# Top-k attention and a Fourier-mixing MLP: the last batch's second chunk in seven products, its folds on one engine, and batch 1's folds spread over one step more

## The chip, the cores and the metric

The kernel runs on one core of a Trainium2 chip. TensorE (PE) multiplies matrices out of on-chip memory (SBUF) into accumulators (PSUM), VectorE (DVE), ScalarE (ACT) and GpSimd (POOL) work elementwise, and SyncE (SP) issues transfers between device memory and SBUF. Every engine takes its own instructions in order; semaphores order them against each other. The metric is the device time of one execution in microseconds. Six runs of the kernel before the change took 1929.75 to 1934.73 us, with a median of 1930.93.

## The reference

Eight batches, eight heads, 576 tokens, head size 64, all in float32; the model width is 8·64 = 512. A top-32 attention feeds a Fourier mixing and an MLP of width 2048:

```python
scores = scale * np.matmul(q, k.transpose(0, 1, 3, 2))
kth = np.partition(scores, -top_k, axis=-1)[..., -top_k:-top_k + 1]
scores = np.where(scores >= kth, scores, -1000000000.0)
attn = softmax(scores)                       # written out with max, exp, sum
x = (attn @ v), heads side by side           # (8, 576, 512)

X = np.fft.fft(np.fft.fft(x, axis=1), axis=2)
u = x + np.real(X)
un = (u - mean(u)) / np.sqrt(var(u) + 1e-06)
return u + np.maximum(un @ w_ch1, 0.0) @ w_ch2
```

## The kernel before, in words

**Steps.** The attention is cut into 288 items: 32 pairs of heads (four per batch), nine items per pair. An item is 128 rows (64 of each of two query tiles' tails in the fifth). A loop over steps `i` writes out every engine's instructions: in step `i` PE makes the scores of item `i+3` and transposes the masked exponentials of item `i-2` (`tpP`, L428); DVE finds the 32 largest of items `i` and `i+1` with MAX8 and MATCH_REPLACE8 (L384, L386); POOL turns the largest and the 32nd into two bounds (`nt`, L393); ACT makes a mask from them (L400), POOL subtracts it (L401), and ACT exponentiates (L407). `attend` (L465) multiplies by v; `to_tokens` transposes the result back (`tpx`, L505, in the single `o` bank of PSUM) and DVE normalises it into the batch's x tile (L509, L516). There are two buffers for x, so batch 2's first x tile waits until batch 0's results have been stored; `to_tokens` is held back in the plan until all four stores are issued.

**A plan by steps.** All that follows attention is put into the step loop by hand, with `at(step, where, function, cost)`. For each batch `T0` is a step two to four after the batch's last item. Then come:

- the folds (`fold_tails`, `fold_ops`): sums and differences of x by symmetry, so that the Fourier transforms are half as long. `fold_ops` has four parts for each parity of the frequency: sums over the token halves (`sd`, L597), over the channel halves (`zw`, L566), and two halves of `fg` (L550 to L562). Batch 0's run on DVE. Batches 1 to 6 fold on POOL (where "pool0"), batch 7 with parity 0 on DVE and parity 1 on POOL.
- the transform over tokens (`dft_tokens`, PE, `yp`, L629), one block for each parity at the steps `ft`; ACT copies it out to `y`.
- the transform over channels (`dft_channels`, PE, `mp`, L677) from step `fc` on, the sum with x, the statistics on DVE (L705, L706), the transposes to channels first (`tpu`, L742) and the inverse root (`rsqrt`).
- the batch's arrival: `mlp_units` puts the MLP into a queue as units. A unit of kind "hidden" multiplies by `w_ch1` (`hp`, L827), followed by a ReLU on ACT; one of kind "back" multiplies by `w_ch2`.

The step loop fills PE with units from that queue. `level` computes, at each arrival, a pace in estimated microseconds a step, such that the queue is empty at the next arrival; in each step units are taken out between the fixed pieces until the pace is met (`some`). The estimates come from `fixed_cost` and the units' costs.

**The MLP in two chunks.** A batch's 576 tokens make chunk 0 (two tiles of 128 and the 64 tail tokens, tile 4) and chunk 1 (tiles 2 and 3). For each tile of 128 the second product is sixteen matmuls 128x512 in eight units (`back`, `cp`, L854); the tails take four units (L893). Chunk 0 of batches 1 to 7 does not work that way. Its two tiles times `w_ch2` are a product of two-by-two blocks, and `fast` computes it with seven block products in place of eight (`p2, p1, p5, p4, p6, p3, p7`, banks `cv` and `cw`, L1025). The sums of blocks of the hidden activations are made by POOL in place (`mix`, L970), those of the weights once at the start, kept in device memory, and brought back over parts of `w_ch2` by SP (`bring`, L770). In the last batch `T4` and `T3` go into the buffers of the attention's `PT` tiles, and each product is added into x by DVE straight from PSUM (`to_x`, L983). `need` writes out a planned POOL sum at the latest where it is used; in the last batch every sum is written out at once.

In the last batch, attention is over when the folds start. What is left in the queue then are 15 units of batch 6's chunk 1.

Of the kernel before, what the change touches and what calls it, by code (L numbers as in the profile page):

```python
# [9 lines left out]
F32 = mybir.dt.float32  # L10
# [8 lines left out]
P = 128  # L19
# [45 lines left out]
def kernel(  # L65
# [9 lines left out]
    nc = tc.nc  # L75
# [10 lines left out]
    NIT = DF // P  # L86
# [9 lines left out]
    CHUNKS = ((0, 1, 4), (2, 3))  # L96
# [9 lines left out]
    attp = ctx.enter_context(tc.tile_pool(name="attp", bufs=2))  # L106
# [654 lines left out]
    DH = DM // 2  # L761
    NK = NIT // 2
# [4 lines left out]
    def bring(o, place, part):  # L767
        kcs = slice(NK // 2 * part, NK // 2 * (part + 1))
        dst = place[part] if isinstance(place, list) else place[:, kcs]
        nc.sync.dma_start(out=dst, in_=scr[:, o, kcs, :])  # L770
# [19 lines left out]
    sums, summed = [], set()  # L790
# [8 lines left out]
    def need(key):  # L799
        if key in summed:  # L800
            return

        kind = next(s[3] for s in sums if s[0] == key)
        for s in [s for s in sums if s[3] == kind]:
            sums.remove(s)
            s[2]()
            summed.add(s[0])
            if s[0] == key:
                break
# [3 lines left out]
    def mlp_units(b):  # L813
# [88 lines left out]
        def tails_done(cp, free):  # L902

            if b and not last:
                need((b, "x", 4))
            ct, rs = ct_of(4), rs_of[b]
            for h in range(2):
                r0 = TAIL + TH * h
                nc.scalar.copy(out=ct[TH * h:TH * (h + 1), :], in_=cp[r0:r0 + TH, :])

            def finish():
                xt, c = x[0:TAIL, 4, :], ct[0:TAIL]
                nc.vector.tensor_tensor(out=c, in0=cp[0:TAIL], in1=c, op=ALU.add)
                free()
                nc.vector.scalar_tensor_tensor(
                    out=xt, in0=c, scalar=rs[0:TAIL, 4:5], in1=xt, op0=ALU.mult, op1=ALU.add
                )
                for h in range(2):
                    tok = HS * h + 2 * P
                    nc.sync.dma_start(  # L920
                        out=out[b, tok:tok + TH, :], in_=x[TH * h:TH * (h + 1), 4, :]
                    )

            if last:
                finish()
            else:
                late_next.append(finish)

        def fast():

            ch = 0
            ta, tb = CHUNKS[ch][0], CHUNKS[ch][1]

            if last:
                second = [
                    attp.tile([P, NK // 2, DH], F32, name=f"w2_s_{n}", tag=f"PT{n}", bufs=1)
                    for n in range(2)
                ]
            else:
                second = w2_21  # L940

            def in_second(kc):
                half = NK // 2
                return second[kc // half][:, kc % half] if last else w2_21[:, kc]
            rs, banks = rs_of[b], {}
            lo, hi = slice(0, DH), slice(DH, DM)

# [10 lines left out]
            def later(key, us, fn, soon=False):  # L958

                n = sum(s[3] for s in sums) if soon else len(sums)  # L960
                sums.insert(n, ((b, *key), us, fn, soon))
                if last:
                    need((b, *key))

            def mix(dst, a, c, op=ALU.subtract):
                v = h()
# [85 lines left out]
                    mix("12", "12", "11")  # L1052

            def p5(part):
                need((b, "21", part))
                c = product("v", hi, "21", first, part, False)
                bring(T2, w2_12, part)
                if part:
                    to_x(tb, hi, c, 2)
# [6 lines left out]
                    mix("22", "22", "11")  # L1066

            def p6(part):
                need((b, "11", part))
                c = product("w", lo, "11", first, part, False)  # L1070
                bring(B12, w2_12, part)
                if part:
                    to_x(ta, hi, c, 4)

            def p3(part):
                need((b, "12", part))
                c = product("v", hi, "12", b22, part, False)
                if part:
                    to_x(ta, hi, c, None, lambda: (banks["v"][1](), store(ta)))

            def p7(part):
                need((b, "22", part))
                c = product("w", lo, "22", in_second, part, False)
                if not last:
                    bring(B21, second, part)
                if part:
                    to_x(tb, slice(0, DM), c, None, lambda: (banks["w"][1](), store(tb)))

            def begin():
# [2 lines left out]
                    if last:  # L1092
                        bring(T4, second, part)

            return [(0.0, begin, "hidden")], [
                (0.0, lambda: mix("21", "21", "22", ALU.add), "back")
            ] + [
                (1.75, lambda f=f, part=part: f(part), "back")
# [4 lines left out]
        for ch in range(2):  # L1103
            units += [
                (8 * CW[ch] / 1200.0, lambda ch=ch, it=it: hidden(ch, it), "hidden")
                for it in range(NIT)
            ]
            if b and ch == 0:
                begin, products = fast()
                units[1:1] = begin  # L1110
                units += products
            for t in (4,) if b and ch == 0 else CHUNKS[ch]:
                units += [
                    (1.75, lambda ch=ch, t=t, p=p: back(ch, t, p), "back")
                    for p in range(4 if t == 4 else 8)
                ]
# [42 lines left out]
    def at(step, where, fn, cost=0.0):  # L1159
        plan.setdefault((step, where), []).append(fn)  # L1160
        costs[step] = costs.get(step, 0.0) + cost
# [74 lines left out]
    for b in range(B):  # L1236
        end = PER_BATCH * (b + 1) - 1
        last = b == B - 1
        first, soon = b == 0, b == 1
        T0 = end + (2 if first else 3 if soon else 4)  # L1240
        if first:

            at(T0 - 1, "pool", lambda b=b: fold_tails(b, nc.gpsimd))

            def folds(b=b):
                for par, space in ((0, "own"), (1, "hT")):
                    for op in fold_ops(b, par, nc.vector, space):
                        op()
            at(T0, "dve", folds)
            ft, fc = (T0 + 1, T0 + 1), T0 + 1  # L1250
        elif soon:

            at(T0 - 1, "pool0", lambda b=b: fold_tails(b, nc.gpsimd))
            for par in range(2):
                def folds(par=par, b=b, T0=T0):
                    for n, op in enumerate(fold_ops(b, par, nc.gpsimd)):
                        at(T0 + 1 + 3 * par + n // 2, "pool0", op)
                at(T0, "begin", folds)
            ft, fc = (T0 + 3, T0 + 6), T0 + 7
        elif not last:  # L1260
            at(T0, "pool0", lambda b=b: fold_tails(b, nc.gpsimd))
            for par in range(2):
                def folds(par=par, b=b, T0=T0):
                    for n, op in enumerate(fold_ops(b, par, nc.gpsimd)):
                        at(T0 + (6 if par else 1) + n, "pool0", op)
                at(T0, "begin", folds)
            ft, fc = (T0 + 5, T0 + 11), T0 + 12
        else:
            at(T0 - 1, "pool0", lambda b=b: fold_tails(b, nc.gpsimd))

            def folds(b=b):
                a = fold_ops(b, 0, nc.vector)
                for op in a + fold_ops(b, 1, nc.gpsimd, "PT"):
                    op()
            at(T0, "dve", folds)
            ft, fc = (T0 + 1, T0 + 3), T0 + 4
        for par in range(2):
            at(ft[par], "pe1", lambda b=b, par=par: dft_tokens(b, par), 4.3)
        for n, t in enumerate((0, 1, 4, 2, 3)):
            quick = first or last  # L1280
            s = fc + (0 if first else n // 3 if last else n // 2)
            at(s, "pe2", lambda b=b, t=t, q=quick: dft_channels(b, t, q), 1.75)
            if not quick:
                at(s, "pool2", lambda b=b, t=t: add_mixed(b, t))
                at(s + 1, "dve", lambda b=b, t=t: stats(b, t))
            at(s + (1 if quick else 2), "pe", lambda b=b, t=t: channels_first(b, t), 0.6)
            if first and t == 4:
                at(s + 1, "pe", lambda: (queue.extend(waiting), waiting.clear()) and 0.0)
        at(s + 1, "begin" if quick else "dve", lambda b=b: rsqrt(b))
        arrivals.append(s + (1 if quick else 2))  # L1290
        at(arrivals[-1], "units", lambda b=b: (queue if b else waiting).extend(mlp_units(b)))
# [28 lines left out]
    def one_unit():  # L1320
        c, fn, _ = queue.pop(0)
        fn()
        return c
# [164 lines left out]
```

## Time and profile before

The profiled execution took 1930.82 us; the profile's span is 1929.0 us, so 1.8 us lie around it.

| | busy us | share of the span | instructions |
|---|---|---|---|
| PE | 1805.4 | 94% | 8960 |
| DVE | 1584.9 | 82% | 3262 |
| ACT | 1208.8 | 63% | 3078 |
| POOL | 871.4 | 45% | 1160 |

| stretch of the span, us | what runs there | PE idle, us |
|---|---|---|
| 320 to 505 | batch 1's attention, batch 0's MLP, batch 1's folds and transforms | 10.5 |
| 505 to 1748 | batches 2 to 7's attention beside the MLP of the batch before | 14.2 |
| 1748 to 1805 | batch 7's folds and transforms, the rest of batch 6's MLP | 5.0 |
| 1805 to 1929 | batch 7's MLP | 4.3 |

How to read what follows. A line of the chain gives start, length, engine, tile and line of a piece of the chain of work that ended last. A line in order of time gives start, length from the first to the last of a group, engine, line, operation, output and input tile, shape and count, and in brackets the idle time ahead of it with what ended it. A line of the windows gives a stretch, its length, the busy time of PE, PE's weight loads, DVE, ACT and POOL, then PE's granted clock as a share of full speed, the transfers' share and their GB/s. A line of the waits gives who waited for whom, the sum in us, how often, and the longest. A matmul in float32 stands in the records as two.

### The profile page before, as it was taken

What the parts mean: (1) busy time and instruction counts of PE and PEld (TensorE: products, weight loads), DVE (VectorE), ACT (ScalarE), POOL (GpSimd) and SP (SyncE); (2) the same over time, 40 slices, a digit from 0 to 9 for tenths busy, and PEclk for the clock granted to TensorE, in tenths of its full rate; (3) what the DMA queues carried; (4) which work ended last, traced back from release to release, by engine and by line L of the source; (5) the groups of instructions that cost most, each with busy time, mean ns of one, the idle gap of its engine ahead of it and who ended that gap; (6) DMA issues with size and microseconds to landing.
All of it is one profiled execution on the core that took longest, in us unless ns stands there. A gap on an engine that the chain in (4) does not pass through costs nothing.

```text
span 1929.0 us, 28145 instructions
## 1 busy us (share of the span) xinstructions
PE 1805.4 (94%) x8960; PEld 1184.1 (61%) x8960; DVE 1584.9 (82%) x3262; ACT 1208.8 (63%) x3078; POOL 871.4 (45%) x1160
## 2 busy tenths in 40 slices
PE   5567699999999999999999999999999999998999
PEld 3334365465666656766567756666567756776675
DVE  8999989999999989989898979998798989852110
ACT  6878657676776667666666657666666657641100
POOL 4767643545534454345525444345435444342010
PEclk8787899999999999999999999999999999999999
DMA  5333002210114101230114101130114101120120
GB/s 163 104 94 106 19 13 63 87 52 24 47 35 115 29 23 38 56 105 19 27 39 128 33 21 38 52 108 20 24 41 121 40 13 52 44 80 6 49 80 11
DMA packets 181652, 107.15 MB, mean 56 GB/s; under 512 B 125825, under 2 KB 172033, under 8 KB 181505
## 3 DMA queue, kind: packets, MB, share of 16 engines
q1 hardware_dynamic: 180720, 105.14, 19.2%
q8 instruction: 72, 1.18, 0.3%
q14 instruction: 76, 0.61, 0.1%
q10 hardware_dynamic: 784, 0.21, 0.0%
HBM read 89.56 MB, written 15.73 MB: 55 GB/s over the span
## 4 chain that ended last, share of the span: by engine, by line
PE 79%; POOL 7%; DVE 7%; issue 3%; ACT 3%; DMA 1%; SPq 0%; POOLq 0%; DVEq 0%; ACTq 0%
PE hp L827 25%; PE cp L854 11%; PE o L465 7%; PE sp L363 6%; PE tpP L428 5%; PE cw L1025 4%; PE cv L1025 4%; PE yp L629 4%; PE mp L677 3%; PE cp L893 3%; DVE m L384 3%; DVE wk L386 2%; POOL wk L401 2%; PE sp_t L333 2%; POOL w L215 1%
## 5 line engine op out<-in xcount | busy, mean ns | idle before, releaser
L401 POOL TENSOR_TENSOR wk<-S,wk 128x576 f32<-128x576 f32 x288 | 407.8, 1416 | 792.8 <-ACT wk L400 771.1
L384 DVE MAX8 m<-wk 128x8 f32<-128x576 f32 x864 | 623.1, 749 | 5.2
L827 PE MATMUL hp<-unT,w 128*128 128x256 f32 (+1 forms) x2048 | 536.6, 409 | 2.1 <-ACT unT L745 2.1
L827 PEld LDWEIGHTS hp<-unT,w 128*128 128x128 f32 x2048 | 372.8, 190 | 124.0 <-issue 21.9
L386 DVE MATCH_REPLACE8 wk<-m,wk 128x576 f32<-128x576 f32 x576 | 427.6, 742 | 0.0
L854 PE MATMUL cp<-w,hT 128*128 128x512 f32 x576 | 268.9, 598 | 2.5 <-ACT hT L881 2.5
L407 ACT ACTIVATE wk<-wk,nt 128x576 f32<-128x576 f32 x288 | 224.6, 780 | 71.7 <-POOL wk L401 70.9
L428 PE MATMUL tpP<-ident,wk 128*128 128x128 f32 x1152 | 183.3, 283 | 71.8 <-ACT wk L407 44.8
L400 ACT ACTIVATE wk<-S,nt 128x576 f32<-128x576 f32 x288 | 226.8, 788 | 33.9 <-POOL nt L393 32.9
L431 ACT COPY PT<-tpP 128x512 f32<-128x512 f32 (+1 forms) x320 | 171.1, 546 | 107.8 <-PE tpP L428 105.2
L428 PEld LDWEIGHTS tpP<-ident,wk 128*128 128x128 f32 x1152 | 140.6, 145 | 145.1 <-ACT wk L407 65.5
L831 ACT ACTIVATE hT<-hp 128x320 f32<-128x320 f32 (+1 forms) x256 | 104.8, 409 | 194.5 <-PE hp L827 191.9
L384 DVE MAX8 m<-S 128x8 f32<-128x576 f32 x288 | 213.9, 743 | 8.5 <-ACT S L337 8.5
L386 DVE MATCH_REPLACE8 wk<-m,S 128x576 f32<-128x576 f32 x288 | 213.6, 742 | 0.0
L465 PE MATMUL o<-PT,v 128*64 128x256 f32 (+3 forms) x1440 | 195.0, 413 | 1.6 <-ACT PT L431 1.5
L366 ACT COPY S<-sp 128x512 f32<-128x512 f32 (+1 forms) x264 | 141.7, 587 | 57.9 <-PE sp L363 57.7
L363 PE MATMUL sp<-kT,qT 64*128 64x512 f32 (+1 forms) x528 | 160.7, 668 | 4.3 <-ACT means L1209 3.3
L854 PEld LDWEIGHTS cp<-w,hT 128*128 128x128 f32 x576 | 100.8, 190 | 104.0 <-issue 98.4
L465 PEld LDWEIGHTS o<-PT,v 128*64 128x64 f32 x1440 | 111.5, 152 | 71.0 <-issue 14.3
L1025 PE MATMUL cw<-w,hT 128*128 128x256 f32 x416 | 99.3, 383 | 2.4 <-issue 1.2
L970 POOL TENSOR_TENSOR hT<-hT 128x512 f32<-128x512 f32 x56 | 71.2, 1273 | 53.0 <-ACT hT L831 45.5
L1025 PEld LDWEIGHTS cw<-w,hT 128*128 128x128 f32 x416 | 75.4, 190 | 19.4 <-issue 6.1
(140 smaller groups left out, 2127.0 us busy)
## 6 DMA issues: line engine op xcount, KB each, us to landing
w<-w_parts SPq DMA_DIRECT2D x78, 512.0 KB, 4.3
space<-in_moe_w_ch_dram SPq DMA_DIRECT2D x32, 512.0 KB, 3.3
nat<-in_q_dram SPq DMA_DIRECT2D x128, 64.0 KB, 2.1
v<-in_v_dram SPq DMA_DIRECT2D x128, 64.0 KB, 2.2
out_dram<-x SPq DMA_DIRECT2D x32, 256.0 KB, 2.1
nat<-in_k_dram SPq DMA_DIRECT2D x124, 64.0 KB, 2.1
w_parts<-w_t SPq DMA_DIRECT2D x8, 512.0 KB, 2.9
nat<-in_q_dram SPq DMA_DIRECT2D x128, 8.0 KB, 1.7
```

Of the source, the lines that this page charges most:

```text
L363: nc.tensor.matmul(sp[r], lhsT=qT[hd, q_cols], rhs=kT[hd, :], start=True, stop=True)
L384: ops.append(lambda src=src, m8=m8: nc.vector.max(out=m8, in_=src))
L386: ops.append(lambda src=src, m8=m8: nc.vector.match_replace(w, m8, src, NEG))
L400: nc.scalar.activation(out=w, in_=Ssb[i], func=AF.Relu, scale=-FAR, bias=Nt[i][:, 1:2])
L401: nc.gpsimd.tensor_tensor(out=w, in0=Ssb.pop(i), in1=w, op=ALU.subtract)
L407: nc.scalar.activation(out=w, in_=w, func=AF.Exp, bias=Nt.pop(i)[:, 0:1], accum_out=den_t[pair % 3][:, c:c + 1],)
L428: nc.tensor.transpose(tp[:, c, :], p_sb[:, k0 + P * c:k0 + P * (c + 1)], ident)
L431: nc.scalar.copy(out=pt[:, NF * he:NF * (he + 1), col:col + w], in_=tp[:, :, o:o + w])
L465: nc.tensor.matmul(o[D * e:D * (e + 1), c0:c1], lhsT=vv[:, c, e, :], rhs=pt[:, 2 * NF if c == NF else NF * e + c, c0:c1], start=(c == 0), ...
L827: nc.tensor.matmul(hp[:, 0:w], lhsT=w1[:, dt, P * it:P * (it + 1)], rhs=unT[:, dt, 0:w], start=(dt == 0), stop=(dt == NDT - 1),)
L854: nc.tensor.matmul(cp, lhsT=hT[:, it, P * n:P * (n + 1)], rhs=w2[:, it, :], start=(it == 0), stop=(it == NIT - 1),)
L1025: nc.tensor.matmul(dst, lhsT=h()[a][:, kc, :], rhs=rhs_of(kc), start=start and kc == 0, stop=kc == NK - 1, skip_group_check=True,)
```

## The change

Three things are changed.

- In the last batch, chunk 1 too goes through `fast`. The function takes the chunk as an argument, its keys in `need` carry the chunk, the buffers for `T4` and `T3` are taken anew, the initial loads (`begin`) stand behind the chunk's first hidden unit as in chunk 0, and `p6` brings the block `B12` back only in chunk 0, since nothing reads it after chunk 1.
- In the last batch, the second parity's folds run on DVE behind the first's, no longer on POOL. Ahead of the first `dft_tokens`, two units are taken out of the queue.
- In batch 1, each parity's folds take three steps in place of two (`sd`, `zw`, both halves of `fg`), and `ft`, `fc` and all that follows from them come one step later: 78, 81 and 82 in place of 77, 80 and 81; the arrival is step 86 in place of 85.

```diff
-        def fast():
-
-            ch = 0
+        def fast(ch):
+
             ta, tb = CHUNKS[ch][0], CHUNKS[ch][1]
 
+            second = w2_21
             if last:
                 second = [
-                    attp.tile([P, NK // 2, DH], F32, name=f"w2_s_{n}", tag=f"PT{n}", bufs=1)
+                    attp.tile([P, NK // 2, DH], F32, name=f"w2_s{ch}_{n}", tag=f"PT{n}", bufs=1)
                     for n in range(2)
                 ]
-            else:
-                second = w2_21
...
-                sums.insert(n, ((b, *key), us, fn, soon))
+                sums.insert(n, ((b, ch, *key), us, fn, soon))
                 if last:
-                    need((b, *key))
+                    need((b, ch, *key))
...
             def p6(part):
-                need((b, "11", part))
+                need((b, ch, "11", part))
                 c = product("w", lo, "11", first, part, False)
-                bring(B12, w2_12, part)
+                if ch == 0:
+                    bring(B12, w2_12, part)
...
-            if b and ch == 0:
-                begin, products = fast()
-                units[1:1] = begin
+            seven = b and ch == 0 or last
+            if seven:
+                begin, products = fast(ch)
+                units.insert(1 - NIT, begin)
                 units += products
-            for t in (4,) if b and ch == 0 else CHUNKS[ch]:
+            for t in [t for t in CHUNKS[ch] if t == 4 or not seven]:
...
                     for n, op in enumerate(fold_ops(b, par, nc.gpsimd)):
-                        at(T0 + 1 + 3 * par + n // 2, "pool0", op)
+                        at(T0 + 1 + 3 * par + min(n, 2), "pool0", op)
                 at(T0, "begin", folds)
-            ft, fc = (T0 + 3, T0 + 6), T0 + 7
+            ft, fc = (T0 + 4, T0 + 7), T0 + 8
...
             def folds(b=b):
-                a = fold_ops(b, 0, nc.vector)
-                for op in a + fold_ops(b, 1, nc.gpsimd, "PT"):
+                for op in fold_ops(b, 0, nc.vector) + fold_ops(b, 1, nc.vector, "PT"):
                     op()
             at(T0, "dve", folds)
+
+            at(T0 + 1, "pe1", lambda: one_unit() + one_unit() if len(queue) > 1 else 0.0)
             ft, fc = (T0 + 1, T0 + 3), T0 + 4
```

More of the change, by code (lines that the diff above doesn't have):

```diff
@@ L904, in tails_done @@
             if b and not last:
-                need((b, "x", 4))
+                need((b, 0, "x", 4))
             ct, rs = ct_of(4), rs_of[b]
@@ L1054, in p5 @@
             def p5(part):
-                need((b, "21", part))
+                need((b, ch, "21", part))
                 c = product("v", hi, "21", first, part, False)
@@ L1075, in p3 @@
             def p3(part):
-                need((b, "12", part))
+                need((b, ch, "12", part))
                 c = product("v", hi, "12", b22, part, False)
@@ L1081, in p7 @@
             def p7(part):
-                need((b, "22", part))
+                need((b, ch, "22", part))
                 c = product("w", lo, "22", in_second, part, False)
@@ L1093, in begin @@
                         bring(T4, second, part)
-            return [(0.0, begin, "hidden")], [
+            return (0.0, begin, "hidden"), [
                 (0.0, lambda: mix("21", "21", "22", ALU.add), "back")
```

## The prediction

> **What bounds the kernel now.** I read the busy slices first. TensorE (PE) is at nine tenths or more from about 500 us to the end; what it idles after 505 us is 14 of 1243 us up to 1748, 5.0 of the next 57 and 4.3 of the last 124 (windows 505–1748, 1748–1805, 1805–1929). So from 505 us on PE's work plus PE's gaps is the time, and an edit counts only by the work, gaps or slow clock it takes from PE. The change touches three places; for each I asked for the view that shows what PE does there.
>
> The end of attention, in the chain of waits (start, length, what):
>
> ```profile
> 1750.48 0.44 DVE x L509
> 1751.01 3.42 DVE sd L597
> 1754.45 3.30 DVE zw L566 x2
> ...
> 1758.89 7.08 PE yp L629 x30
> 1765.97 8.58 PE cp L854 x20
> 1774.56 4.00 PE yp L629 x30
> 1778.56 1.73 PE mp L677 x8
> ```
>
> PE is on the chain until the last x tile, then VectorE (DVE) folds for 8 us, then PE again. Two equal blocks of 30 yp records take 7.08 and 4.00 us. The windows say why (the figure ahead of the last two columns is PE's granted clock):
>
> ```profile
> 1754.00:1756.00 2.00, 0.00 (x0) 0.00 (x0) 1.97 (x2) 0.00 (x0) 2.00 (x2) 1.00 0.00 0
> 1758.00:1760.00 2.00, 1.11 (x4) 1.11 (x5) 2.00 (x4) 0.00 (x0) 2.00 (x3) 0.51 0.00 0
> 1762.00:1764.00 2.00, 2.00 (x8) 0.97 (x8) 0.00 (x0) 0.26 (x1) 0.00 (x0) 0.50 0.00 0
> ```
>
> PE idles 5 us and returns at half clock. Meanwhile GpSimd (POOL) is busy: it folds the other parity. Batch 0's folds, on DVE alone, take a third of the time for the same shape (DVE in order of time):
>
> ```profile
> 232.25 1.23 DVE L597 TENSOR_TENSOR sd<-x 128x1024 f32<-128x1024 f32 x1
> 233.50 1.29 DVE L566 TENSOR_TENSOR zw<-sd 128x512 f32<-128x512 f32 x2
> ```
>
> The last batch's second phase, PE in order of time: the seven products of chunk 0 (16 records each; one matmul is two records), and the plain products of chunk 1.
>
> ```profile
> 1852.46 3.69 PE L1025 MATMUL cw<-w,hT 128*128 128x256 f32 x16 [0.62 <-issue]
> 1855.98 3.62 PE L1025 MATMUL cv<-w,hT 128*128 128x256 f32 x16
> 1897.73 27.63 PE L854 MATMUL cp<-w,hT 128*128 128x512 f32 x64
> ```
>
> Batch 1's folds: who PE waited for between 465 and 500 us, and POOL's order of time.
>
> ```profile
> PE yp L629 <- POOL fg L550: 2.7, 1, 2.7
> PE tpP L428 <- ACT wk L407: 2.4, 1, 2.4
> PE tpq L277 <- ACT PT L431: 1.1, 1, 1.1
> ```
>
> ```profile
> 477.07 1.40 POOL L401 TENSOR_TENSOR wk<-S,wk 128x576 f32<-128x576 f32 x1 [3.93 <-PE sp_t L333]
> 478.43 2.37 POOL L597 TENSOR_TENSOR sd<-x 128x1024 f32<-128x1024 f32 x1
> 480.87 2.51 POOL L566 TENSOR_TENSOR zw<-sd 128x512 f32<-128x512 f32 x2
> 483.34 0.19 POOL L393 TENSOR_TENSOR nt<-m,cc 128x2 f32<-128x2 f32 x1
> ```
>
> The tiny `nt`, from which ScalarE (ACT) masks, POOL subtracts, ACT exponentiates and PE transposes, stands behind 4.9 us of folds.
>
> **B. Last batch's folds.** Removed from POOL: ten instructions (1750.99–1761.5). Added to DVE, which was idle 1761.5–1780.4: the same ten behind parity 0's. Moved on PE: two units (four matmuls, 8 records, 3.44 us) from behind the first yp block to ahead of it. No DMA is among them. With POOL quiet I price a parity by batch 0: 232.25 to 237.40 is 5.15, the next to 242.67 is 5.27. So parity 0 is ready at 1751.01+5.15 = 1756.2 and parity 1 at 1761.4. PE runs cp from 1750.28 for 8+8 records, 6.88, to 1757.2: the folds are in by then, by 1.0 us. Then yp 4.01 at full clock, 12 records of cp 5.15 (8.58·12/20), yp 4.01: 20.05 from 1750.28. Before, the same work ran to the mp at 1778.40: 28.12. Gain 8.1: 5.2 of gap, 2.9 of slow clock. Parity 1 is needed at 1766.3 and is 4.9 early; ACT's evictions of y and the mp follow the second yp block as before.
>
> Bounds: nothing more than the 8.1 can go. If DVE keeps 3.4 us for such a fold even alone, yp starts at 1758.9 as before, but after a gap of 1.7; the gaps of 2.4 and 2.7 near 480 us left the clock at 1.00 in the 10-us windows there, so it runs at full speed, bounded by its second half's fold at 1761.4 (about 1763.3); cp to 1768.5; parity 1's first half 10.5 us behind parity 0's 1758.9, at 1769.4; yp ends by 1773.7, a gain of 4.7. I take 8.1, since 232.25's row is the same engine and shape with POOL out of the folds.
>
> The Trainium skill ("GPSIMD Engine Reference", Specifications) says that POOL shares its SBUF interfaces with DVE, in contention when a DVE instruction has two SBUF inputs. The rows agree: 3.42 beside POOL's sd, 1.23 without it. By that rule the folds get the short price and the sum is 8.1; left out, the long price and 4.7 would do as well.
>
> The skill ("TensorE: Matmul & The Clock Gate", What's actually happening) halves the clock after an idle window of about 3.4 us that runs free of the kernel. The 5-us gap at half clock agrees; a 1.7-us gap should not trip it. It speaks against the edit in one way: if the folds came much later than priced, the clock would drop again and 2.9 us would come back.
>
> **A. Chunk 1 of the last batch in seven products.** Removed: 32 matmuls 128x512 (64 records) and two DVE adds of 0.75. Added: 56 matmuls 128x256, eight POOL sums (1.27 each; POOL is idle there), six DVE adds of 0.48 and one of 0.75, eight 512-KB loads on SP's queue; two loads of chunk 0's kind are not repeated. Chunk 0 did just this from 1837.86 to 1862.98: 25.12, with its waits in it (0.62, and about 0.2 inside the next block, for the T2 loads, which take 4.9 us to land after p5 frees their place). Chunk 1 took 27.63. Gain 2.5. The first four loads are issued behind the tails' stores (1872.9), over 30 us ahead of p5; the POOL sums run beside p2, p1 and p3 as in chunk 0. After the last matmul stand an add of 0.75 and one 256-KB store, as before. Bounds: without the two waits 3.3; with them doubled 1.7. I take chunk 0's own row.
>
> **C. Batch 1, one step more.** Nothing is added. POOL's folds now stand one of sd, zw, fg per step in steps 75–80 (before: sd with zw in 75 and 78, fg in 76 and 79), so `nt` waits behind 2.4–2.9 us instead of 4.9. The yp blocks move from steps 77 and 80 to 78 and 81, mp, POOL's adds, stats, tpu and the units' arrival (85 to 86) one later. The planner's pace falls from 5.14 to 5.06 in steps 39–85 and rises from 5.32 to 5.42 in 86–126: one unit (1.7) is done later. From step 127 on the pace is the same, so C's effect is the PE gap won or lost before.
>
> What goes: the loop nt, mask (0.86), subtract (1.40), folds, nt was 7.5 us with sd and zw; it becomes 5.0 to 5.4, near DVE's own 5.1 a step (MAX8 at 454.27, 459.35, 464.43). So the wait of 2.4 on the exponential and most of the 2.7 and 1.1 should go; DVE's own 1.6 (for PE's transposes behind yp) goes as yp leaves that step. What is late next: in step 81 PE reaches yp about a microsecond before POOL's last fg; batch 0's last tile ends two steps later, its store stands behind step 81's eight k loads (5 us of SP), and batch 2's first x tile waits for that store, moving from step 81 to 84, so that step 85's tpx waits for DVE to empty the one `o` bank (such waits cost 1.2 in all now). And one more step without units: DVE needs 5.1, PE has 2.2 of its own work. Bounds: all 6.2 won; or nothing won and 2.9 lost. I take 6.2 less about 1.5 and 1.2 for the two late ones: 3.5 won.
>
> **Sum.** 8.1 + 2.5 + 3.5 = 14.1. The profiled execution took 1930.8 (span 1929.0 and 1.8 around it), 0.1 under the median of the runs. 1930.9 − 14.1 = 1916.8.
>
> **Rivals.** (1) C loses: the step without units starves PE by 2.9 and the old waits stay in other places. For: PE had no unit left from 476 us on. Against: PE was fully busy from 500 us, so it was behind, not starved. 1930.9 − 8.1 − 2.5 + 2.9 = 1923.2. (2) DVE folds slowly alone: 1930.9 − 4.7 − 2.5 − 3.5 = 1920.2. For: batch 0's rows had a COPY of 1.24 among them, so DVE was not wholly undisturbed. Against: the sd and zw rows. (3) Slower: SP's loads in the last chunk are not hidden. p6 and p7 need the four halves of T2 and T3; each that lands bare costs 4.9. Without waits A wins 3.3, and all the rest 11.6, so three bare halves (14.7) break even and four give 1930.9 − 14.9 + 19.6 = 1935.6. Against: chunk 0's same loads cost 0.9 in all, with two more loads in the queue.
>
> **How the numbers follow.** Forecast 0.70, (1) 0.18, (2) 0.07, (3) 0.05. A measurement tells 0.2% (3.9 us) from no change, so below 1927.0 is faster. Forecast and (2) are faster, (1) is mostly so but could cost twice its price or slow the 86 re-ordered steps further: 0.04 of it within 0.2%; (3) is slower. Faster 0.90, same 0.05, slower 0.05. Range: low with all of C (6.2), A without waits (3.3), 8.1: 1913.3, written 1913.0; high at rival (1), 1923.2, rounded out for jitter in the re-ordered steps to 1923.5.
>
> **What would show it.** B: DVE sd near 1.2, no gap ahead of yp, clock 1.00 throughout, both yp blocks 4.0. A: seven blocks near 3.45 at the end, gaps under 1 us. C: no wait of PE over 2 us between 465 and 515, first hp of batch 1 a step later at about the same time. The number is wrong if PE idles more than now between 320 and 520 us, or if gaps appear in batches 2 to 6, where the order of PE's instructions is unchanged.

## The result, and the profile after

The changed kernel took 1925.16 us (median of 17 runs, 1922.08 to 1928.84). The kernel before took 1930.61 us beside it (37 runs). The ratio is 0.9972, with a 95% interval of 0.9966 to 0.9979, so the change is 5.45 us faster. The forecast was 1916.8 us, with a range of 1913.0 to 1923.5. The direction was right, and the time is 1.7 us above the range.

The profiled execution of the changed kernel took 1923.47 us, with a span of 1921.6. The profile is read here at the same places as before the change.

The end of attention, in the changed kernel's chain of waits (start, length, what):

```profile
1753.37 0.22 PE tpx L505 x2
1753.59 6.87 PE cp L854 x16
1760.46 4.00 PE yp L629 x30
1764.46 5.15 PE cp L854 x12
1769.61 4.00 PE yp L629 x30
1773.61 1.73 PE mp L677 x8
```

DVE has left the chain. Sixteen records of `cp` stand ahead of the first `yp` block, and both blocks of `yp` take 4.00 us. From `tpx` to `mp` it is 20.24 us, against 28.33 us in the kernel before (1750.23 to 1778.56): 8.09 us less, where 8.1 was forecast. The changed kernel's windows at the places of the old gap and the old slow clock (length, busy time of PE, weight loads, DVE, ACT, POOL, then the granted clock):

```profile
1757.00:1759.00 2.00, 2.00 (x6) 0.81 (x5) 2.00 (x6) 0.00 (x0) 0.00 (x0) 1.00 0.00 0
1761.00:1763.00 2.00, 2.00 (x16) 1.44 (x15) 1.38 (x5) 0.19 (x1) 0.00 (x0) 1.00 0.00 0
```

PE is busy throughout, at full clock, and POOL does nothing. The same fold on DVE, in order of time:

```profile
1754.15 1.23 DVE L597 TENSOR_TENSOR sd<-x 128x1024 f32<-128x1024 f32 x1
1755.41 1.29 DVE L566 TENSOR_TENSOR zw<-sd 128x512 f32<-128x512 f32 x2
```

These are 1.23 and 1.29 us, as in batch 0's rows. The last batch's chunk 1, PE in order of time:

```profile
1903.14 3.62 PE L1024 MATMUL cw<-w_s,hT 128*128 128x256 f32 x16
1907.38 3.69 PE L1024 MATMUL cw<-w,hT 128*128 128x256 f32 x16 [0.62 <-issue]
...
1914.37 3.62 PE L1024 MATMUL cw<-w_s,hT 128*128 128x256 f32 x16
```

The seven products run from 1892.94 to 1918.0: 25.1 us in place of the 27.5 that the plain products take in the chain of the kernel before, with the same single wait of 0.62 as in chunk 0. That is 2.4 us, where 2.5 was forecast.

So A and B came as priced, and what is missing is in batch 1's stretch. Who PE waited for between 440 and 515 us, in the changed kernel:

```profile
PE tpP L428 <- ACT wk L407: 5.9, 2, 3.7
PE yp L629 <- POOL fg L550: 0.4, 1, 0.4
PE tpq L277 <- ACT PT L431: 0.3, 1, 0.3
```

Of the three waits that the prediction named, two shrank: the wait on `fg` from 2.7 to 0.4 and the one on `PT` from 1.1 to 0.3. The one on the exponential stayed, 2.3 after 2.4. And a new wait of 3.7 us stands in the first line. It starts at 457 us, one step before the moved folds begin. From there to the end of attention the changed kernel stays behind: its first `hp` of batch 1 starts at 517.97 us, against 513.54, and its last `tpx` at 1753.37, against 1750.23.

### The profile page after: what moved, and what is told of

Read it like the earlier page. It is cut to its first block, busy times and chain, and to the rows that moved or that the text cites. A ratio compares the mean times of both kernels' runs of the same rounds, so it can differ in the third digit from the quotient of the medians.

```text
span 1921.6 us, 28279 instructions
## 1 busy us (share of the span) xinstructions
PE 1800.6 (94%) x9008; PEld 1193.0 (62%) x9008; DVE 1584.7 (82%) x3277; ACT 1208.6 (63%) x3078; POOL 871.3 (45%) x1158
## 3 DMA queue, kind: packets, MB, share of 16 engines
q1 hardware_dynamic: 183408, 109.33, 19.9%
## 4 chain that ended last, share of the span: by engine, by line
PE 79%; POOL 8%; ACT 4%; issue 3%; DVE 3%; DMA 1%; SPq 0%; POOLq 0%; DVEq 0%; ACTq 0%
PE hp L827 25%; PE cp L854 10%; PE o L465 7%; PE sp L363 6%; PE tpP L428 5%; PE cw L1024 5%; PE cv L1024 4%; PE yp L629 3%; PE mp L677 3%; PE cp L893 3%; POOL wk L401 3%; POOL w L215 2%; POOL w L214 2%; PE sp_t L333 2%; DVE m L384 1%
## 5 line engine op out<-in xcount | busy, mean ns | idle before, releaser
L827 PEld LDWEIGHTS hp<-unT,w 128*128 128x128 f32 x2048 | 373.7, 191 | 124.2 <-issue 24.2
L854 PE MATMUL cp<-w,hT 128*128 128x512 f32 x512 | 241.5, 599 | 4.0 <-ACT hT L881 4.0
L854 PEld LDWEIGHTS cp<-w,hT 128*128 128x128 f32 x512 | 88.5, 190 | 91.5 <-issue 84.7
L969 POOL TENSOR_TENSOR hT<-hT 128x512 f32<-128x512 f32 x64 | 81.5, 1275 | 101.2 <-ACT hT L831 89.4
L1024 PE MATMUL cw<-w,hT 128*128 128x256 f32 x448 | 106.5, 383 | 2.7 <-issue 1.4
L1024 PEld LDWEIGHTS cw<-w,hT 128*128 128x128 f32 x448 | 81.4, 190 | 20.3 <-issue 5.2
```

The lines of the kernel that those rows point to most:

```text
L827: nc.tensor.matmul(hp[:, 0:w], lhsT=w1[:, dt, P * it:P * (it + 1)], rhs=unT[:, dt, 0:w], start=(dt == 0), stop=(dt == NDT - 1),)
L854: nc.tensor.matmul(cp, lhsT=hT[:, it, P * n:P * (n + 1)], rhs=w2[:, it, :], start=(it == 0), stop=(it == NIT - 1),)
L1024: nc.tensor.matmul(dst, lhsT=h()[a][:, kc, :], rhs=rhs_of(kc), start=start and kc == 0, stop=kc == NK - 1, skip_group_check=True,)
```

## The experiments

All medians are set against the kernel before on the same chip.

| run | what | median, us | against before, us | ratio and 95% interval |
|---|---|---|---|---|
| the change | A, B and C | 1925.16 | −5.5 | 0.9972 [0.9966, 0.9979] |
| e1_ab | A and B | 1920.92 | −9.9 | 0.9951 [0.9939, 0.9964] |
| e2_c | C alone | 1935.78 | +5.0 | 1.0028 [1.0018, 1.0037] |
| e3_shift | the change, folds over two steps | 1924.84 | −6.0 | 0.9969 [0.9959, 0.9980] |
| e4_pace | the change, first pace 5.14 | 1919.84 | −11.0 | 0.9948 [0.9934, 0.9962] |
| e5_pace506 | A and B, first pace 5.06 | 1924.32 | −7.4 | 0.9958 [0.9945, 0.9970] |
| e6_defer | the change, one POOL sum later | 1921.60 | −10.1 | 0.9948 [0.9936, 0.9961] |
| e7_nounits | A and B without the two units | 1922.36 | −9.3 | 0.9949 [0.9936, 0.9961] |
| e8_pool | A and B, parity 1 on POOL | 1923.47 | −8.2 | 0.9956 [0.9942, 0.9969] |
| e9_pace526 | the change, first pace 5.26 | 1931.64 | +0.9 | 1.0002 [0.9993, 1.0011] |

Three more runs (l1_after, l2_after, l3_pace506) are single executions, taken for their profiles. The interval of a row with five runs is some ±2.5 us wide, so two such rows that differ by less are not told apart.

### Which part failed: the change without C, and C alone

The first run takes C out of the change; the second puts C alone, the same lines the other way round, into the kernel before.

```diff
-                        at(T0 + 1 + 3 * par + min(n, 2), "pool0", op)
+                        at(T0 + 1 + 3 * par + n // 2, "pool0", op)
-            ft, fc = (T0 + 4, T0 + 7), T0 + 8
+            ft, fc = (T0 + 3, T0 + 6), T0 + 7
```

> The change without C: batch 1's folds and transforms stay at their old steps; the last batch's two edits are in. Theory P (C costs, A and B give what was predicted): 10.6 us under the kernel before, about 1920.0. Theory Q (A and B give less than their rows say, C gives nothing): about 5.4 us under it, as the whole change.

A and B without C give 9.9 us, where the sum of their terms was 10.6.

> The kernel before with C alone. Theory P: about 5 us slower than the kernel before (the whole change's gain of 5.4 less the 10.6 of A and B), with a wider spread of the runs than before. Theory Q: within 1 us of it. The prediction's own term would make it 3.5 us faster.

C alone makes the kernel 5.0 us slower, and its nine runs spread over 1931.75 to 1939.4, against 1928.95 to 1932.67 of the kernel before. C was forecast to win 3.5. What follows is about C.

### Which half of C: the spread of the folds, the shift, or the pace

C does three things: it spreads each parity's folds over three steps, it moves the transforms a step on, and, because the arrival moves from step 85 to 86, it lowers the planner's pace in steps 39 to 85 from 5.14 to 5.06. The first experiment takes the spreading back and keeps the other two.

```diff
-                        at(T0 + 1 + 3 * par + min(n, 2), "pool0", op)
+                        at(T0 + 1 + 3 * par + n // 2, "pool0", op)
```

> The whole change, but with batch 1's folds in two steps a parity as before (sum and difference with channel halves in one step); transforms and arrival still one step later. It tells what the spreading of the folds is worth by itself. If the spreading works as predicted, this is 2 to 4 us slower than the whole change (the bounds wait behind 4.9 us of folds again). If the shift alone makes C's loss and the spreading does nothing: the same time as the whole change, within 1 us.

1924.84 us, the same as the whole change; the wait of 3.66 is there too. The spreading is not what costs. It does not win the expected 2 to 4 us either: from 465 to 520 us PE idles 5.0 us here and 3.6 in the change, so it is worth 1.4 there.

Why the wait on the exponential stayed can be read from ACT and POOL in order of time. The kernel before:

```profile
472.95 0.19 POOL L393 TENSOR_TENSOR nt<-m,cc 128x2 f32<-128x2 f32 x1
476.14 0.86 ACT L400 ACTIVATE wk<-S,nt 128x576 f32<-128x576 f32 x1
```

The changed kernel:

```profile
478.18 1.41 POOL L401 TENSOR_TENSOR wk<-S,wk 128x576 f32<-128x576 f32 x1 [0.88 <-ACT wk L400]
480.78 0.66 ACT L431 COPY PT<-tpP 128x256 f32<-128x256 f32 x2
482.11 0.77 ACT L407 ACTIVATE wk<-wk,nt 128x576 f32<-128x576 f32 x1
```

Before, `nt` is done three microseconds ahead of the mask that reads it, and ACT has no idle time from 470.73 to the mask: copies of `kT`, `y` and `PT` stand ahead of it. After, POOL's subtraction ends at 479.59 and the exponential starts at 482.11, again behind copies of `y` and `PT`. So in both kernels this wait comes from the `yp` block and ACT's copies around it, and not from `nt` standing behind POOL's folds, which is what the spreading removes. This is read from the traces; no run moves ACT's copies.

The next experiment keeps spread and shift, and holds the pace where it was.

```diff
-            step_us = level(i)
+            step_us = 5.14 if i == arrivals[0] else level(i)
```

> The whole change, with the planner's pace for steps 39 to 85 held at the 5.14 of the kernel before in place of 5.06, so that PE's order up to step 76 is that of before. If C's loss comes from the re-paced order of steps 39 to 77 (theory P1): 3 to 5 us faster than the whole change, about 1921. If it comes from the one more step without MLP units ahead of the arrival, or from the steps after it (theory P2): within 1 us of the whole change.

1919.84 us, 5.5 us better against the kernel before than the change. The long wait at 457 us is gone. The prediction's first rival held a further step without units to be what C costs. PE's last unit ahead of the arrival starts at 474.24 us in the kernel before, at 487.52 in the changed kernel and at 468.31 in e4_pace: the changed kernel is not without units for longer, and e4_pace, which is, loses nothing. So that rival had the sign of C's term and not its cause.

### How a pace makes a wait of 3.7 us

The pace decides between which fixed pieces the units stand. PE in order of time, the kernel before:

```profile
445.06 1.98 PE L854 MATMUL cp<-w,hT 128*128 128x512 f32 x4
...
448.82 0.60 PE L428 MATMUL tpP<-ident,wk 128*128 128x128 f32 x4
```

And the changed kernel:

```profile
448.31 0.60 PE L428 MATMUL tpP<-ident,wk 128*128 128x128 f32 x4
448.75 0.27 PE L439 MATMUL tpP_t<-ident,wk 128*128 128x128 f32 x1
448.86 1.88 PE L854 MATMUL cp<-w,hT 128*128 128x512 f32 x4
...
460.65 0.66 PE L428 MATMUL tpP<-ident,wk 128*128 128x128 f32 x4 [3.66 <-ACT wk L407]
```

Each shows the eighth and last `cp` unit of batch 0's tile 2 (the first starts at 423.20 before and at 427.99 after). At the lower pace it stands behind `tpP` and no longer ahead of it. ACT scales that product (L881) at 451.63 in place of 448.15, behind an exponential that itself waits. POOL's sum of it, L883, follows; POOL in order of time, the kernel before:

```profile
449.57 1.28 POOL L883 TENSOR_TENSOR x<-x,hT 128x512 f32<-128x512 f32 x1
450.81 1.41 POOL L566 TENSOR_TENSOR zt<-x 64x256 f32<-64x256 f32 x2
...
454.42 0.18 POOL L393 TENSOR_TENSOR nt<-m,cc 128x2 f32<-128x2 f32 x1
```

The changed kernel:

```profile
452.38 1.27 POOL L883 TENSOR_TENSOR x<-x,hT 128x512 f32<-128x512 f32 x1 [1.55 <-ACT hT L881]
453.61 1.40 POOL L566 TENSOR_TENSOR zt<-x 64x256 f32<-64x256 f32 x2
...
457.23 0.18 POOL L393 TENSOR_TENSOR nt<-m,cc 128x2 f32<-128x2 f32 x1
458.30 1.40 POOL L401 TENSOR_TENSOR wk<-S,wk 128x576 f32<-128x576 f32 x1 [0.89 <-ACT wk L400]
```

POOL waits 1.55 us for ACT, and behind the sum stand the folds of the tails (3.6 us) and then the tiny `nt`. `nt` comes 2.8 us later; ACT's mask waits for it, POOL's subtraction for the mask, ACT's exponential for that, and PE's next `tpP` for the exponential. One unit that slipped behind one block of transposes has become 3.66 us of PE.

That is a reading of two traces. The test leaves the pace at 5.06 and moves only POOL's sum behind `nt`:

```diff
-                        nc.gpsimd.tensor_tensor(out=xt, in0=xt, in1=ct, op=ALU.add)
+                        add = lambda: nc.gpsimd.tensor_tensor(out=xt, in0=xt, in1=ct, op=ALU.add)
+                        at(now[0], "pool", add) if b == 0 and t == 2 else add()
```

> The whole change with its pace of 5.06; only POOL's sum of batch 0's tile 2 (L883) is written out at the end of its step, behind the folds of the tails and behind nt, in place of ahead of them. The order of PE, DVE, ACT and SP is unchanged. Theory P (POOL's sum, waiting for ACT's late scaling, holds the folds and nt back): the wait of PE of 3.66 us for the exponential falls under 1.5 us, and the time falls by 2.5 to 3.5 from the changed kernel's 1925.0, to 1921.5 to 1922.5, more if the clock was lowered by that wait in part of the runs; the spread of the runs falls to some 2 us. Rival R (nt would be late all the same, or the next item in POOL's queue takes the place): the wait stays over 2.5 us and the time at 1924 to 1925.5.

POOL in order of time, PE's `tpP` at the place of the long wait, and the waits of PE between 440 and 515 us, in this run:

```profile
452.61 0.19 POOL L393 TENSOR_TENSOR nt<-m,cc 128x2 f32<-128x2 f32 x1
452.76 1.27 POOL L883 TENSOR_TENSOR x<-x,hT 128x512 f32<-128x512 f32 x1
454.17 1.41 POOL L401 TENSOR_TENSOR wk<-S,wk 128x576 f32<-128x576 f32 x1
```

```profile
456.53 0.66 PE L428 MATMUL tpP<-ident,wk 128*128 128x128 f32 x4 [1.34 <-ACT wk L407]
```

```profile
PE tpP L428 <- ACT wk L407: 3.6, 2, 2.3
```

The wait of 3.66 has become 1.34, and the kernel stands at −10.1 in place of −5.5 us. One POOL instruction, moved behind eleven others in its queue, brings back 4.6 us in the medians. That is more than the 2.3 by which the wait shrank; the two intervals, which do not meet, are wide enough to allow 2.3 too, and the next section but one tells what may make up the rest. One part of the expectation failed: the five runs spread over 5.4 us (1919.76 to 1925.2), not 2.

### The pace alone, and another pace

> The edits A and B without C, and the planner's pace at its first arrival set to 5.06 in place of the computed 5.14; no fold and no transform of batch 1 is moved. A and B alone took 1920.9 us. Theory P (the lower pace is what costs: it lets the last unit of batch 0's tile 2 fall behind the transposes of step 73, so that ACT's scaling, POOL's sum and then POOL's nt come late and PE waits over 3 us for the exponential near 457 us): 1924 to 1926.5 us, with that wait of 3.5 in the trace and the old waits of 2.3 to 2.7 us near 480 still there. Theory Q (the pace costs only together with the shifted folds and transforms): 1920 to 1922, no wait over 3 us. If P holds and the long wait is also what spreads the runs, the runs spread over 4 us or more, as they do with C; if the shift spreads them, over 2 us.

The edit is e4's line with 5.06 in it, in the kernel with A and B only. The wait is there (3.67 us), and so is one of 3.03 near 478 us. The median stands 2.5 us behind e1_ab against the kernel before, but the intervals overlap. Of the old waits, the one on `fg` is gone: PE comes later. Theory P's wait is shown, its price is not: the two profiled executions of this kernel, 1920.45 and 1920.11 us, have the long wait and are as fast as e1_ab's, 1920.28. From 520 to 1700 us they idle 9.4 us where e1_ab idles 13.3; no run tells why. The four other times of e5_pace506 are 1924.1 to 1925.5, and none of those executions was profiled.

If a lower pace hurts, does a higher one help?

> The whole change with the pace of the first arrival set to 5.26 in place of the computed 5.06 (5.14 gave 1919.84, and the computed one some 1925). At 5.26 batch 0's tile 2 is finished and its POOL sum stands two items earlier in POOL's queue, and the queue of units is empty at step 76 in place of 80. Theory P (the loss of the changed kernel comes from POOL's late sum ahead of the folds and from what else the order at 5.06 happens to put late): no wait of PE over 3 us between 430 and 480 us, 1918.5 to 1921.5 us. Rival R (a pace above the level is bad in itself: the queue runs empty early, steps without units follow in which PE waits for VectorE's 5.1 us): one to two such steps more, waits of 2.9 each between 470 and 510 us, 1922.5 to 1926.

It doesn't: 1931.64 us, slower than both theories had it, and 11.9 us behind the pace of 5.14 against the kernel before. Who PE waited for between 340 and 500 us in this run:

```profile
PE tpP L428 <- ACT wk L407: 6.9, 5, 2.8
PE tpP L428 <- ACT kT L287: 3.9, 1, 3.9
```

Units are used up at step 76. The wait of 3.9 is at 476 us, in a step that has none left: ACT's copy of `kT` stands behind a mask that waits for POOL's `nt`, and PE has nothing to put in between. So theory P's place for the loss was not the only one, and rival R has the direction, at about twice the upper end of its price. This profile also has five stretches at half clock between 255 and 510 us, where e4_pace's has one; the next section prices one at 1.7 us. PE's idle time by stretches, taken from the windows (length less busy time, us):

| stretch | before | e1_ab | the change (l1_after) | e6_defer | e4_pace | e9_pace526 |
|---|---|---|---|---|---|---|
| 270 to 320 | 0.2 | 0.2 | 2.1 | 2.1 | 0.2 | 0.4 |
| 320 to 465 | 3.8 | 3.8 | 7.2 | 5.0 | 3.8 | 4.7 |
| 465 to 520 | 6.7 | 6.7 | 3.6 | 3.6 | 5.4 | 9.7 |
| 520 to 740 | 3.0 | 2.9 | 3.3 | 3.2 | 2.3 | 2.7 |
| 740 to 1700 | 10.4 | 10.5 | 10.4 | 10.6 | 8.2 | 8.2 |
| sum | 24.2 | 24.1 | 26.6 | 24.5 | 19.9 | 25.7 |

The change against e1_ab is C: 3.2 us won in 465 to 520, and 5.4 lost ahead of the moved folds. With C, paces of 5.06, 5.14 and 5.26 give 26.6, 19.9 and 25.7: the idle time does not follow the pace up or down, each order has its own long waits. Of the 6.7 us between the change and e4_pace, 5.4 lie ahead of 465 us and 3.2 behind 520, where no run tells the cause; 1.9 go the other way between. e9_pace526 idles 5.8 us more than e4_pace and has four more stretches at half clock; together these make 12.6 of the 14.6 us between the two profiled executions.

### Why the runs spread, and why a gap costs more than itself

The changed kernel's 17 times fall into two groups: eleven between 1922.1 and 1925.4, six between 1927.1 and 1928.8. Two more executions of it were profiled, with no edit, and one more of e5_pace506.

> The changed kernel as it is, one more profiled execution, to see another of the times between 1922 and 1929 from the inside. Theory K (clock: after a gap of PE of over 2 us the granted clock falls to 0.50 for some 3.4 us in some executions and not in others, and each such stretch costs 1.7; the changed kernel has four gaps over 2 us ahead of 500 us, the longest 3.66): the stretches of PE at 0.50 behind the gaps at 259, 348, 457 and 480 us differ from those of the first profile (one, at 260), and their number times 1.7 accounts for the difference of the two executions to within 1 us. Rival L (the gaps themselves change, by transfers that land later): the same clock, other gaps.

> The same once more: theory K as before, with the count of stretches at half clock times 1.7 us accounting for the time against the other two profiles; rival L, other gaps at the same clock.

> A and B with the pace of 5.06 alone, one more profiled execution. Four of its five times were 1924.1 to 1925.5 and the profiled one 1920.45, with one stretch at half clock, behind the gap of 3.0 at 478 us. Theory K: this execution, if it takes 1924 or more, has two or more further stretches at 0.50 of some 3.4 us, one of them behind the gap of 3.67 at 456 us. Rival L: other gaps, the same clock.

They took 1922.28, 1928.06 and 1920.11 us. The windows of l1_after (the third figure from the right is the granted clock):

```profile
260.00:265.00 5.00, 3.91 (x15) 2.80 (x16) 4.93 (x11) 1.48 (x4) 3.90 (x15) 1.00 0.00 0
350.00:355.00 5.00, 5.00 (x23) 2.51 (x19) 4.93 (x11) 4.24 (x13) 3.02 (x5) 1.00 0.40 141
460.00:465.00 5.00, 5.00 (x15) 1.98 (x14) 4.93 (x11) 1.99 (x6) 3.87 (x3) 1.00 0.00 0
485.00:490.00 5.00, 4.66 (x24) 2.39 (x20) 4.97 (x12) 3.99 (x12) 3.67 (x7) 1.00 0.00 0
```

The same program in l2_after:

```profile
260.00:265.00 5.00, 4.69 (x11) 3.11 (x12) 4.93 (x11) 0.70 (x2) 4.10 (x14) 0.66 0.00 0
350.00:355.00 5.00, 5.00 (x22) 2.49 (x21) 4.93 (x11) 3.69 (x9) 2.19 (x4) 0.66 0.46 159
460.00:465.00 5.00, 3.28 (x9) 1.66 (x10) 4.81 (x11) 3.26 (x9) 3.28 (x4) 0.80 0.00 0
465.00:470.00 5.00, 5.00 (x13) 1.84 (x12) 4.93 (x11) 1.24 (x3) 1.50 (x2) 0.86 0.00 0
485.00:490.00 5.00, 4.20 (x20) 2.20 (x22) 4.93 (x11) 3.10 (x8) 3.31 (x5) 0.69 0.00 0
```

PE's gaps are the same in both (the longest is 3.7 us in both). The clock is not: behind each of four gaps (2.08, 1.92, 3.68 and 2.28 us) l2_after runs at half speed for some 3.4 us, and l1_after never does. What one such stretch costs is seen in the same sixteen records of `hp` behind the gap at 259 us; first the kernel before, at full clock:

```profile
261.11 4.57 PE L827 MATMUL hp<-unT,w 128*128 128x320 f32 x16 [2.08 <-ACT unT L745]
```

then the changed kernel's first profile, with a half-speed stretch there:

```profile
260.44 6.26 PE L827 MATMUL hp<-unT,w 128*128 128x320 f32 x16 [2.08 <-ACT unT L745]
```

6.26 − 4.57 = 1.69. Four stretches make 6.8 us, and the two executions differ by 5.8: theory K, to within the 1 us that it gave itself, and rival L (other gaps) is out. The rest is in the start: these records of `hp` begin at 261.09 us in l1_after, 260.44 in the first profile and 260.31 in l2_after. From there to the end of the span the three take 1659.4, 1661.2 and 1666.0 us, so one stretch costs 1.8 and four cost 6.6. The execution of l3_pace506 is not above 1924, so for e5_pace506 the point stays open; it had one half-speed stretch, near 482 us.

This is also the rest of C's price. The change in l1_after and e1_ab in its profile are both without such a stretch from 255 us on: 1922.28 and 1920.28, so C's gaps alone cost 2.0 us. In the medians C costs 4.4 (−9.9 against −5.5); the other 2.4 are put down to half-speed stretches of 1.7 each in the unprofiled executions, which is an inference from the three profiles. The long gap's share in these was not measured by itself; e6_defer, which cuts it, wins 2.5 us between executions without such stretches (1919.76 against 1922.28), and 4.6 in the medians.

### The two halves of B

From the kernel with A and B, the two units are left out:

```diff
-            at(T0 + 1, "pe1", lambda: one_unit() + one_unit() if len(queue) > 1 else 0.0)
```

> A and B without C (1920.9 us), less the two units taken out of the queue ahead of the last batch's first transform; both parities' folds stay on DVE. PE then has two units less, 3.44 us, to run while DVE folds. Theory B1 (what matters is only that the folds come in before PE has run out, and that a gap under some 3 us leaves the clock alone): DVE is done 4.7 us after the last tpx and PE has 3.4 us of work, a gap of about 1.3, full clock, 1921.9 to 1922.7 us. Theory B2 (the units are what keeps the clock up): a gap of 1.3 and yp at half clock for some us, 1924 to 1925.5.

or the second parity goes back to POOL:

```diff
-                for op in fold_ops(b, 0, nc.vector) + fold_ops(b, 1, nc.vector, "PT"):
+                for op in fold_ops(b, 0, nc.vector) + fold_ops(b, 1, nc.gpsimd, "PT"):
```

> A and B without C (1920.9 us), but the second parity's folds on POOL again beside DVE's; the two units stay ahead of the first transform. Theory B1: DVE's folds take 8 us again beside POOL's, PE has 6.9 us of work, a gap of about 1.6 and full clock: 1922.2 to 1923.0 us, so either half of B alone gets most of its gain. Theory B2 (POOL's and DVE's folds side by side cost more than the gap, or the clock falls): 1924.5 to 1926.

The waits of PE between 1740 and 1800 us, e7_nounits:

```profile
PE yp L629 <- DVE fg L550: 0.3, 1, 0.3
```

and e8_pool:

```profile
PE yp L629 <- DVE fg L550: 1.6, 1, 1.6
```

Against the kernel before these are −9.3 and −8.2 us, where both halves together make −9.9. Without the units a wait of 0.3 is left (1.3 was expected: `yp` starts on the first half of `fg` and doesn't need the second yet). With POOL beside it, DVE's folds are slow again, as its order of time in e8_pool shows,

```profile
1752.47 3.40 DVE L597 TENSOR_TENSOR sd<-x 128x1024 f32<-128x1024 f32 x1
```

but the two units cover all but 1.6 us of it, and the clock stays at 1.00 behind that gap:

```profile
1760.00:1762.00 2.00, 1.64 (x12) 1.57 (x12) 2.00 (x4) 0.00 (x0) 2.00 (x3) 1.00 0.00 0
```

The gaps and the clock are as theory B1 has them, though e8_pool's 1923.47 lies 0.5 above its range. That a gap under some 3 us leaves the clock alone, as B1 also says, is shown here by one execution with a gap of 1.6, and does not hold in general: in l2_after gaps of 1.92 to 2.28 us were followed by half clock. From the last `tpx` to `mp` the chain takes 20.24 us with both halves (e1_ab), 20.78 without the units, 22.21 with POOL's folds, and 28.33 in the kernel before. Either half of B thus removes most of the 8.1 us, since what costs is a gap of five microseconds with the half clock behind it, and either half shortens it enough; the second half adds 0.5 or 2.0.

## Why the prediction was wrong, point by point

- **B, 8.1 us: right.** 8.09 in the profile, by the steps given: DVE's fold at 1.23 us and no gap ahead of `yp`, both blocks at full clock. A whole parity took 4.07 us where 5.15 was priced, which changes nothing, as PE had work until later. e8_pool shows the cause of the short fold as well, by putting POOL's folds back: 3.40 us for the same instruction in the same place. The rival of slow folds on DVE alone is out.
- **A, 2.5 us: right.** 2.4, with one wait of 0.62 as in chunk 0. The rival of SP's loads laid bare is out. Together A and B gave 9.9 of 10.6 in the medians.
- **C, the wait part: right in part.** "So the wait of 2.4 on the exponential and most of the 2.7 and 1.1 should go": they went from 6.2 to 3.0 in the changed kernel's waits, and the stretch 465 to 520 idles 3.2 us less. But the 2.4 was read wrongly: it is a wait for ACT's copies around `yp`, not for folds ahead of `nt`, and it stayed at 2.3, against the prediction's own sign (no wait over 2 us between 465 and 515). At the old pace (e4_pace) the three are 2.3, 1.1 and 1.1, so spread and shift take 1.7 of the 6.2 there; the lower pace leaves PE a unit in these steps (487.52), which covers more. The late `yp` of step 81 costs 0.4 and not a microsecond. The wait for the `o` bank, priced at 1.2, is not there: no `tpx` waits between 505 and 540 us.
- **C, the failed step.** The prediction saw that the pace falls from 5.14 to 5.06 in steps 39 to 85, and costed it as "one unit (1.7) is done later". That counts work and not order. The lower pace moves units against the fixed pieces in all these steps, and ahead of the folds the new order has 5.4 us more of gaps: the 3.66 behind POOL's late sum, 1.5 us near 303 and 1.9 in place of 0.6 near 348 are the largest, against 1.3 won near 355. This stood in the prediction as a possibility ("slow the 86 re-ordered steps further: 0.04") and had no price, while a C with "3.5 won" was the likeliest case. C's gaps cost 2.0 us net, where 3.5 were to be won. Holding the pace (e4_pace) or moving the one late sum (e6_defer) takes the loss away.
- **Clock, the second term that was missing.** "The gaps of 2.4 and 2.7 near 480 us left the clock at 1.00" was true of that one execution. In others the same place had the half clock (e8_pool: 0.66 in 480 to 485, behind a gap of 2.5), at 1.7 us each. By the account above it brings C to 4.4 us in the medians. The Trainium skill ("TensorE: Matmul & The Clock Gate", What's actually happening) has windows of about 3.4 us that run free of the kernel, and half clock after an idle one. The length of the stretches, some 3.4 us, agrees with that. But here gaps of 1.9 to 2.3 us, much shorter than such a window, were enough in some executions, and the measurement decides.
- **Rival 1** (C loses 2.9) had the sign, and its 1923.2 is nearer than the forecast, but it put the loss on a step without units. The changed kernel has no more of these, e4_pace has, and e4_pace loses nothing. So the nearness is luck.
- The sum with C as e2_c measured it by itself, 1930.9 − 8.1 − 2.5 + 5.0 = 1925.3, is within 0.2 us of the result.

e4_pace, with C at the old pace, and e6_defer are the best kernels, at 0.9948; e1_ab, without C, has 0.9951. C at its best is thus worth nothing that these runs can tell.

## What to carry to other kernels

Where a planner spreads fill-in work by a level, moving one due time re-orders everything up to it: compare the order of instructions on each engine over the whole planned stretch, and look for a late producer that has come to stand ahead of a small, urgent instruction in an in-order queue. Price a gap on PE as its length plus a chance of 1.7 us of half clock (here from gaps of 1.92 us on; one of 1.6 had none in its one profile), and don't take the clock behind a gap from one execution. Look at the part of the change that is "only moved" with the same care as at the parts that remove work: here it ate 4 us of the 10 that the others won.

## What the runs showed that was not expected

- The same gaps in the same program give a half-speed stretch of some 3.4 us or none: the gap of 2.08 at 259 us had 1.00 behind it in the profile of the kernel before and 0.66 over five microseconds in the changed kernel's first. In l2_after four gaps of four had it, in l1_after none.
- The kernel before has gaps of 2.1, 2.4 and 2.7 us too, and its times hardly spread. e8_pool, whose order ahead of the last batch's folds is the same, was hit twice in its profile, behind gaps of 2.1 and 2.5 us. Why the executions of the kernel before are rarely hit is open.
- A DVE fold of 128x1024 takes 1.23 us alone and 3.40 beside POOL's folds, in two kernels (e1_ab and e8_pool) that differ only in the engine of the other parity's folds.
